# Batch 2 loaded transposed through memory, six output tiles split into half sums, and a new written order in a one-core attention + MLP kernel

## The chip, the cores and the metric

The kernel runs on one core of a Trainium2 chip. The metric is the device time of one execution in microseconds. One execution was also taken with the hardware profiler, and all the profile lines come from it. The engines are named as the profile names them: PE (TensorE, matrix products), PEld (its weight loads), DVE (VectorE), ACT (ScalarE), POOL (GpSimd, which here issues the casting loads) and SP (SyncE, which issues stores and transposed loads).

## The reference, cut to what matters

```python
# q, k, v: (8 batches, 12 heads, 448 positions, 64); w_in: (768, 2048); w_out: (2048, 768), all float32
scores = (1.0 / np.sqrt(64)) * np.matmul(q, k.transpose(0, 1, 3, 2))
m = np.max(scores, axis=-1, keepdims=True)
e = np.exp(scores - m)
attn = e / (np.sum(e, axis=-1, keepdims=True) + np.exp(-m) + 1e-09)
x = np.matmul(attn, v).transpose(0, 2, 1, 3).reshape(3584, 768)   # heads side by side
h = np.maximum(x @ w_in, 0.0)
out = (h * h) @ w_out                                             # (3584, 768) float32
```

The softmax has one more term, exp(0), in its denominator. The kernel computes exp(scores) without the maximum and adds 1 to the sum instead, which is the same quotient.

## The kernel before, in words

All matrix products are in float16, with sums in float32 in PSUM. Batches are worked on one after the other, and within a batch heads are taken four at a time, in a "quad": three quads a batch.

For each batch the kernel needs q and k with the head dimension on the partitions (tile `qk`, two buffers), so that scores come out with keys on partitions. There are two ways to get them:

- Batches in `ON_PE` (here 0, 1 and 2): POOL loads a quad of q and k in its natural layout, casting to float16 (`load_quad`, tiles `nn`); PE transposes it (`transpose_one`, 14 PE transposes a step, written `T b,g,n`); DVE or ACT copies the result to `qk` (`transposed_copy`, written `U`).
- The later batches: POOL copies all q and k of the batch to float16 tensors in device memory (`stage`), SP then loads them with a transposing DMA (`transposed_loads`, three planes: q, k, and k shifted by one row), and POOL picks the last 64 keys of every head out of the planes (`tail_keys`, four small copies).

In the second way the positions of a batch lie in another order, so `quad_scores` runs eight 64x64 products of 224 columns for a step instead of four of 448, `load_v_quads` takes four DMAs instead of one or three, and `store` writes rows with step 2 instead of 7.

A quad then goes through seven score steps (`s`), seven exps on ACT (`e`), DVE additions for the sums (`a`), a product with ones (`S`), logarithm and exp on ACT for the reciprocal (`Z`, `M`), seven products with the values (`v`), and two multiplications on DVE (`X`), which give x with its 768 features on the partitions (`xt`). Batch 0 does the same in halves of 224 queries (`p`, `b`, `y`, `z`, `n`, `x`, with `t`/`u`/`T`/`U` ahead of it).

The hidden layer takes x against w_in in 16 blocks of 128 features (`i` for batch 0 in pairs of blocks and halves of queries, `j` later), a relu on ACT or DVE (`r`, `k`), and a squaring on DVE (`g`, `l`) into the ring `gs`. An output tile is 128 tokens by 384 columns: 16 products of `gs` with w_out (`o`), then a scaled copy from PSUM (`O`) and a store on SP. `out_piece` has two forms: one 128x128 product a block, or (rows=True) four 64x64 products, whose two half sums lie in two PSUM banks, `op` and `lo`; then `out_first` (`O`) copies the one and `out_second` (`Q`, DVE, L563) adds the other.

Tile scheduling is by hand: the order of the instructions on every engine is the written one. It is a list of steps: `ORDER` (L662) for batches 0 to 2 with the first six output tiles (EARLY = 6), then `CYCLE` (L719) run five times for the later batches, then a tail of plain loops. Each engine takes its instructions in that order and waits where its data or its buffer is not ready. So a step that waits holds back all that stands behind it on its engine. That is so for the queues too: SP's stores and transposed loads are in one order, and POOL's loads, stage copies and tail copies are in one order.

The step `d n` issues `LOADS[n]` (L614). In `ORDER` of before these are the quads of batches 0, 1 and 2, the values, four parts of w_in, four of w_out, `stage(3)`, and `load_third` (transposed loads, tail copies and values of batch 3, `stage(4)`). In `CYCLE` a single `d0` near its end issues the transposed loads, tail copies and values of the next batch and the stage copies of the one after (`following`).

PSUM has two pairs of banks for scores (`s_psum`), and from the step `P0` on a ring of four banks (`ring`), which hidden-layer blocks, value products and output tiles take in turn. Output tiles in `ORDER` take one bank of it, those in `CYCLE` two. `osb_pool` has four buffers for copied output tiles.

Of the kernel before, what the change touches and what calls it, by code (L numbers as in the profile page):

```python
# [10 lines left out]
FP16 = mybir.dt.float16  # L11
# [5 lines left out]
def kernel(  # L17
# [9 lines left out]
    nc = tc.nc  # L27

    B, H, S, D = q.shape
# [4 lines left out]
    RUN = 4  # L34
    NQ = H // 4
    KC = S // 64
    ON_PE = (0, 1, 2)
    COLS = H * S // 2 + 16
    HALF = DM // 2
    FIRST = S // 2  # L40
# [11 lines left out]
    flat = ctx.enter_context(tc.tile_pool(name="flat", bufs=2))  # L52
# [90 lines left out]
    def stage(b):  # L143
        for n, t in (("q", q), ("k", k)):
# [11 lines left out]
            if hi < lo + TOTAL:  # L156
                nc.gpsimd.dma_start(out=st[hi - lo:TOTAL].rearrange("(r w) -> r w", r=1),
                                    in_=src[0:lo + TOTAL - hi].rearrange("(r w) -> r w", r=1))

    def transposed_loads(b):  # L160
        qk = qks[b] = qk_pool.tile([128, 3, COLS], FP16, name="qk")
        for i, n, x, c in ((0, "q", FRONT, H * S // 2), (1, "k", FRONT, H * S // 2), (2, "k", 0, COLS)):
            nc.sync.dma_start(
                out=qk[:, i, 0:c],
                in_=stages[n, b][x:x + c * 2 * D].rearrange("(r c) -> r c", c=2 * D),
                transpose=True,
            )

    kms = {}

    def tail_keys(b):

        km = kms[b] = flat.tile([128, H, 64], FP16, name="flatq")
        for r in range(2):
            for odd in range(2):
                rows_ = slice(64 * r, 64 * r + 64)
                which, x = (1, 0) if odd == r else (2, odd)
                src = qks[b][rows_, which, x:x + H * S // 2].rearrange("p (h x) -> p h x", h=H)
                nc.gpsimd.tensor_copy(km[rows_].rearrange("p h (x o) -> p h x o", o=2)[:, :, :, odd],  # L179
                                      src[:, :, S // 2 - 32:S // 2])  # L180
# [3 lines left out]
    def qk_of(b):  # L184
        if b not in qks:
            qks[b] = qk_pool.tile([128, 3, COLS], FP16, name="qk")
        return qks[b]
# [378 lines left out]
    def out_done(tok, n0, w, act=True):  # L566
        out_first(tok, n0, w, act)
        ot = ots.pop((tok, n0))
        del ops[tok, n0]
        store(tok, ot, n0, n0 + w)  # L570
# [28 lines left out]

    def load_quad(b, g):  # L600

        x = {(0, 1): (0, 0), (0, 2): (0, 1), (1, 0): (1, 0), (1, 1): (0, 0), (1, 2): (0, 1),
             (2, 0): (1, 0), (2, 1): (1, 1), (2, 2): (0, 0)}[b, g]
        if (b, x[0]) not in nats:
            nats[b, x[0]] = nat.tile([128, RUN * 2 * S], FP16, name=f"nn{x[0]}")
        load_natural_quads(b, (g,), x[1], nats[b, x[0]])

    def load_third():
        transposed_loads(3)
        tail_keys(3)  # L610
        load_v_quads(3)
        stage(4)

    LOADS = ([lambda b=b, g=g: load_quad(b, g) for b in range(3) for g in range(NQ) if b + g]  # L614
             + [lambda b=b, g=g: load_v_quads(b, g, g + 1) for b in range(2) for g in range(NQ)]
             + [lambda: load_v_quads(2)]
             + [lambda i=i: load_win(i, NW) for i in range(NW)]
             + [lambda n0=n0, y=y: load_wout(n0, y, 2) for n0 in (0, HALF) for y in range(2)]
             + [lambda: stage(3), load_third])

    def quad_visit(n):
        return divmod(n - N0, KC)
# [28 lines left out]
        "v": lambda m, c: values_step(m, c),  # L651
        "X": lambda m: quad_x(m),
        "P": lambda n: other_ring(),
        "o": lambda n, f0, f1: out_piece(128 * (n // 2), HALF * (n % 2), HALF, range(f0, f1)),
        "O": lambda n, act: out_done(128 * (n // 2), HALF * (n % 2), HALF, act),
    }

    def other_ring():
# [1 line left out]
        ring.append(ctx.enter_context(tc.tile_pool(name="ring", bufs=4, space=bass.MemoryType.PSUM)))  # L660

    ORDER = """  # L662
        d0 W8 c1,4,0 c0,0,1 c1,0,1 t0,0,0 c0,4,1 t1,0,0 u0,0,0,0 t1,0,4 u1,0,0,0 t0,0,4 u1,0,4,0 s0 d8 d1 u0,0,4,0 t0,1,0 e0 t1,1,0 u0,1,0,0 u1,1,0,0 s1 s2 e1
        d10 t0,1,4 u0,1,4,0 t1,1,4 u1,1,4,1 T0,1,0 T0,1,1 s3 U0,1,0,0,4,0 e2 U0,1,1,0,4,0 s4 U0,1,0,4,7,1 e3 d9 U0,1,1,4,7,0 d2 p0 e4 p2 s16 p1 e16 b0,0 b0,1
        p3 b0,2 b0,3 s6 y0 d18 s5 T0,2,0 e6 U0,2,0,0,4,0 z0 T0,2,1 U0,2,1,0,4,0 e5 U0,2,1,4,7,0 U0,2,0,4,7,0 s7 s9 b1,0 n0 b1,1 e7 x0 s8 p4 e9 b1,2 d3 b1,3 p5
        e8 p6 p7 s10 y1 b2,0 p8 p9 e10 s11 p10 b2,1 z1 e11 b2,2 b2,3 s12 p11 s13 n1 x1 y2 e12 T1,0,0 U1,0,0,0,7,0 T1,0,1 z2 n2 s14 e13 x2 p12 p13 s15
        U1,0,1,0,7,0 e14 e15 s17 p14 b3,0 b3,1 e17 s18 i0,7 d17 d5 b3,2 e18 b3,3 p15 y3 z3 b4,0 r0,7,0 s21 s19 e21 T1,1,1 d4 n3 b4,1 i0,6 U1,1,1,0,7,0 s20 d15
        T1,1,0 x3 b4,2 e19 b4,3 d16 s23 p16 p17 p18 r0,6,0 U1,1,0,0,7,0 e20 b5,0 e23 s22 e22 b5,1 p19 y4 s26 z4 n4 i0,4 g0,7 x4 r0,4,0 s27 i0,5 g0,6 b5,2 e26
        s25 e27 T1,2,1 s28 e25 p20 p21 r0,5,0 p22 s24 g0,5 b5,3 e28 d11 T1,2,0 p23 e24 s29 y5 e29 U1,2,1,0,7,0 U1,2,0,0,7,0 T2,0,0 T2,0,1 U2,0,0,0,7,0 z5 g0,4
        d6 U2,0,1,0,7,0 s30 n5 s32 a0,0 e30 d13 i0,0 i0,1 s33 x5 e32 r0,0,0 g0,0 r0,1,0 s31 i1,0 d12 g0,1 e33 i0,3 r1,0,0 e31 r0,3,1 s35 d7 s36 e35 P0 e36  # L670
        i0,2 s34 e34 a0,1 a0,2 g1,0 v0,0 a0,3 S0 v0,1 v0,2 v0,3 v0,4 Z0 v0,5 v0,6 M0 r0,2,0 g0,3 g0,2 s37 i1,3 a1,0 a1,1 e37 X0 r1,3,0 a1,2 g1,3 i1,6 s39 s40
        a1,3 e39 i1,1 r1,1,0 r1,6,0 s43 T2,2,0 e40 d20 T2,2,1 g1,6 e43 s42 g1,1 e42 U2,2,0,0,7,0 s41 d19 i1,5 r1,5,0 e41 s38 e38 T2,1,0 T2,1,1 U2,2,1,0,7,0
        U2,1,0,0,7,1 S1 a2,0 Z1 s44 U2,1,1,0,7,0 i1,4 i1,2 a2,1 e44 r1,4,1 s45 a2,2 g1,5 a2,3 v1,0 v1,1 M1 v1,2 v1,3 v1,4 v1,5 v1,6 r1,2,1 v2,0 S2 v2,1 X1
        g1,4 e45 g1,2 v2,2 v2,3 v2,4 Z2 v2,5 v2,6 M2 s47 X2 s46 i1,7 j3,0,2 r1,7,0 o0,0,4 j3,2,4 j1,0,2 j3,4,6 k3,0 j12,0,2 o0,4,8 j1,2,4 o0,8,12 e46 e47
        o0,12,16 s50 d21 g1,7 s51 j12,2,4 j1,4,6 k1,0 j5,0,2 e51 e50 l3 j5,2,4 j5,4,6 d23 O0,1 k5,1 j12,4,6 l5 o1,0,4 s48 s49 j6,0,2 e49 l1 e48 d22 k12,1 l12
        o1,4,8 o1,8,12 o1,12,16 s53 s52 e52 e53 j6,2,4 j10,0,2 o5,0,4 j6,4,6 O1,1 s55 k6,0 s54 j10,2,4 o5,4,8 j0,0,2 e55 a3,0 j10,4,6 j8,0,2 o5,8,12 j0,2,4
        a3,1 k10,1 o5,12,16 e54 s61 s57 l6 a4,0 j14,0,2 O5,0 e57 j14,2,4 j14,4,6 e61 j8,2,4 a3,2 j9,0,2 j9,2,4 j0,4,6 j9,4,6 a3,3 j8,4,6 l10 s56 k0,0 k14,0
        e56 l0 k8,1 s58 o2,0,4 o2,4,8 l14 d14 s59 v4,0 v4,1 v4,2 v4,3 a4,1 v4,4 v4,5 e58 k9,0 s60 e59 s64 o2,8,12 d24 l9 o2,12,16 a4,2 a4,3 j7,0,2 e60 v4,6
        e64 S4 Z4 M4 O2,0 S3 j7,2,4 o4,0,4 l8 o4,4,8 o4,8,12 o4,12,16 j7,4,6 Z3 s62 X4 s63 M3 O4,0 v3,0 v3,1 v3,2 v3,3 v3,4 v3,5 e62 v3,6 s65 X3 k7,1 j4,0,2
        e65 o3,0,4 a5,0 o3,4,8 o3,8,12 o3,12,16 j15,0,2 j4,2,4 j4,4,6 l7 e63 j15,2,4 a5,1 j2,0,2 O3,1 a5,2 j2,2,4 a5,3 j15,4,6 k4,0 j13,0,2 j11,0,2 S5 Z5  # L680
        k15,0 M5 l4 l15 j2,4,6 k2,0 j13,2,4 l2 j11,2,4 j13,4,6 j11,4,6 k11,1 k13,1 l11 l13
    """

    for step in ORDER.split():
# [4 lines left out]
    def cycle(b):  # L689
        m = NQ * (b - 1) - 1  # L690
        first = EARLY + KC * (b - 3)

        def following():
            if b + 1 < B:
                transposed_loads(b + 1)
                tail_keys(b + 1)
                load_v_quads(b + 1)
                if b + 2 < B:
                    stage(b + 2)

        return {
# [11 lines left out]
            "o": lambda n, f0, f1: out_piece(128 * ((first + n) // 2), HALF * ((first + n) % 2), HALF, range(f0, f1), True),  # L713
            "O": lambda n, act: out_first(128 * ((first + n) // 2), HALF * ((first + n) % 2), HALF, act),
            "Q": lambda n: out_second(128 * ((first + n) // 2), HALF * ((first + n) % 2), HALF),
            "d": lambda n: following(),
        }

    CYCLE = """  # L719
# [71 lines left out]
```

## Time and profile before

| | us |
|---|---|
| median of 3 runs | 396.94 (395.67 to 397.16) |
| the profiled execution | 396.87 |
| its span, first to last instruction | 394.8 |
| granted TensorE clock | 1.00 of full speed |
| ORDER ends (first value products of the first cycle) | 105.9 |
| five cycles, from one's first value products to the next's | about 45.2, one of them 46.3 |
| POOL waiting for transposed planes, ten waits | 205.6 |
| planes of batch 3: first issue, last plane landed | 83.6, 95.6 |

How to read it: the span is cut by the page into 40 slices of 9.9 us; a digit is the busy share of a slice in tenths. In a timeline a line gives the start, the length, the engine, the line of the kernel, the operation with its tiles and shapes, and how many instructions are merged; a bracket gives idle time ahead of it and what ended it. Matmuls overlap in the pipeline, so the length of one (about 0.32 us) is not its price; the price shows in the starts of a row of them. A window's line gives busy time of each engine, then the clock, the share of the DMA engines (above 1 when packets overlap) and GB/s.

### The profile page before, as it was taken

How to read it: one execution, taken by the hardware profiler on the slowest of the kernel's cores; microseconds unless marked ns; L12 is line 12 of the kernel's file. 1: busy time of each engine (PE TensorE's matmuls, PEld its weight loads, DVE VectorE, ACT ScalarE, POOL GpSimd, SP SyncE). 2: the span in 40 equal slices, each digit the busy share in tenths (PEclk: the TensorE clock that was granted, in tenths of full speed). 3: DMA queues.
4: the chain of work that ended last, by engine and by line, in shares of the span. 5: the costliest groups of instructions: out<-in, count | busy, mean ns of one | idle time of the engine just before them, and what ended most of it. 6: DMA issues, size and time to landing. Idle time of an engine off the chain costs nothing.

```text
span 394.8 us, 13877 instructions
## 1 busy us (share of the span) xinstructions
PE 385.5 (98%) x6252; PEld 262.9 (67%) x6252; DVE 240.5 (61%) x445; ACT 238.1 (60%) x324; POOL 59.8 (15%) x96
## 2 busy tenths in 40 slices
PE   8789999999999999999999999999999999999997
PEld 4567776445599766896579866776677765555665
DVE  3889994385746765668536876567646785285000
ACT  4999895768479625895279834896269934100111
POOL 8354500003200032000500016000500000000000
PEclk9999999999999999999999999999999999999999
DMA  8999999568942579419692398527652100100222
GB/s 146 203 204 206 203 206 208 98 127 154 191 85 63 113 140 181 96 43 161 113 203 75 77 193 127 129 64 141 126 74 68 58 7 2 62 0 14 68 80 81
DMA packets 75051, 45.33 MB, mean 115 GB/s; under 512 B 47472, under 2 KB 72944, under 8 KB 74992
## 3 DMA queue, kind: packets, MB, share of 16 engines
q0 software_dynamic: 24752, 22.62, 36.3%
q1 hardware_dynamic: 49952, 21.59, 25.0%
q8 instruction: 49, 0.80, 0.8%
q10 hardware_dynamic: 288, 0.23, 0.2%
q14 instruction: 10, 0.08, 0.1%
HBM read 45.69 MB, written 17.93 MB: 161 GB/s over the span
## 4 chain that ended last, share of the span: by engine, by line
PE 94%; DVE 3%; ACT 1%; issue 1%; DVEq 0%; ACTq 0%
PE mp L92 81%; PE sp L92 9%; PE xp L92 2%; PE mp L198 2%; ACT et L245 1%; DVE qk L208 1%; DVE half L334 1%; DVE half L332 0%; PE mp L225 0%; ACT rcp L356 0%; ACT rcp L363 0%; DVE qk L235 0%; DVE half L338 0%; DVE half L336 0%; DVE rt L496 0%
## 5 line engine op out<-in xcount | busy, mean ns | idle before, releaser
L92 PE MATMUL mp<-wout,gs 64*64 64x384 f16 (+2 forms) x2592 | 166.7, 322 | 0.0
L92 PE MATMUL mp<-xt,win 128*64 128x448 f16 (+2 forms) x1344 | 151.4, 339 | 0.1
L245 ACT ACTIVATE et<-sp 128x896 f16<-128x896 f32 (+1 forms) x131 | 110.8, 889 | 30.1 <-PE sp L92 28.9
L92 PEld LDWEIGHTS <-win 128*64 128x64 f16 (+1 forms) x1344 | 89.6, 106 | 58.7 <-issue 7.4
L92 PEld LDWEIGHTS <-gs 64*64 64x64 f16 (+1 forms) x2592 | 105.9, 106 | 34.3 <-issue 1.1
L494 ACT ACTIVATE rt<-mp 128x448 f16<-128x448 f32 x55 | 29.3, 544 | 57.2 <-PE mp L92 52.4
L500 DVE TENSOR_TENSOR gs<-rt 128x448 f16<-128x448 f16 x128 | 49.2, 401 | 22.2 <-ACT rt L494 19.8
L92 PE MATMUL sp<-qk 64*64 64x224 f16 (+1 forms) x1056 | 57.4, 274 | 2.5 <-issue 0.9
L496 DVE TENSOR_SCALAR rt<-mp 128x448 f16<-128x448 f32 x73 | 45.2, 621 | 23.0 <-PE mp L92 21.5
L557 ACT ACTIVATE ot<-mp 128x384 f32<-128x384 f32 (+2 forms) x34 | 16.4, 481 | 51.3 <-PE mp L92 50.8
L92 PEld LDWEIGHTS <-qk 64*64 64x64 f16 x1056 | 36.1, 114 | 14.4 <-issue 7.4
L179 POOL COPY flatq<-qk 64x384 f16<-64x384 f16 x20 | 12.4, 643 | 205.9 <-DMA qk<-stage_k 205.6
L245 ACT ACTIVATE nn<-sp 128x896 f16<-128x896 f32 x42 | 36.7, 915 | 1.9 <-PE sp L92 1.8
L478 DVE TENSOR_TENSOR xt<-mp,rcp 128x448 f16<-128x448 f32 x42 | 24.3, 620 | 20.0 <-ACT rcp L457 17.8
L92 PEld LDWEIGHTS <-vn 64*64 64x64 f16 x756 | 24.1, 107 | 9.8 <-issue 2.6
L563 DVE SCALAR_TENSOR_TENSOR ot<-mp,ot 128x384 f32<-128x384 f32 x35 | 19.5, 556 | 16.9 <-ACT ot L557 15.3
L454 ACT ACTIVATE rcp<-sp,one_b 128x896 f32<-128x896 f32 x21 | 21.2, 1007 | 10.0 <-PE sp L92 10.0
L92 PE MATMUL mp<-et,vn 64*64 64x448 f16 (+1 forms) x448 | 25.1, 343 | 0.0
L559 DVE TENSOR_SCALAR ot<-mp 128x384 f32<-128x384 f32 x23 | 12.8, 556 | 19.6 <-PE mp L92 19.5
L432 DVE TENSOR_TENSOR half<-et 128x1792 f16<-128x1792 f16 x15 | 16.3, 1087 | 7.0 <-ACT et L245 6.9
L457 ACT ACTIVATE rcp<-rcp 128x896 f32<-128x896 f32 x21 | 20.0, 952 | 0.6
L434 DVE TENSOR_TENSOR half<-half,et 128x1792 f16<-128x1792 f16 x15 | 16.4, 1091 | 0.7 <-ACT et L245 0.3
(59 smaller groups left out, 198.2 us busy)
## 6 DMA issues: line engine op xcount, KB each, us to landing
out_dram<-ot SPq DMA_DIRECT2D x52, 96.0 KB, 2.3
out_dram<-ot SPq DMA_DIRECT2D x19, 192.0 KB, 1.9
win<-in_moe_w_in_dram POOLq DMA_DIRECT2D x8, 384.0 KB, 11.1
wout<-in_moe_w_out_dram POOLq DMA_DIRECT2D x4, 768.0 KB, 15.6
vn<-in_v_dram POOLq DMA_DIRECT2D x10, 288.0 KB, 4.8
stage_q<-in_q_dram POOLq DMA_DIRECT2D x4, 676.0 KB, 8.8
stage_k<-in_k_dram POOLq DMA_DIRECT2D x4, 676.0 KB, 12.0
nn<-in_q_dram POOLq DMA_DIRECT2D x8, 224.0 KB, 8.1
```

The source lines that it names most:

```text
L92: return nc.tensor.matmul(out_, lhsT, rhs, start=start, stop=stop)
L245: nc.scalar.activation(out=out_, in_=in_, func=AF.Exp, scale=scale)
L432: nc.vector.tensor_add(esq[m], a[:, 0:w], a[:, w:2 * w])
L434: nc.vector.tensor_add(esq[m], esq[m], z[:, 0:w])
L454: nc.scalar.activation(out=rcp, in_=zp[:, :, 0:S], func=AF.Ln, bias=one_b)
L457: nc.scalar.activation(out=zqs[m], in_=zqs[m], func=AF.Exp, scale=-1.0)
L478: nc.vector.tensor_mul(xts[b][:, 2 * g + i, :], xqs[m][i][:, 0:S], zqs[m][:, i, :])
L494: nc.scalar.activation(out=rt[:, 0:m], in_=hp[:, 0:m], func=AF.Relu)
L496: nc.vector.tensor_scalar(out=rt[:, 0:m], in0=hp[:, 0:m], scalar1=0.0, scalar2=None, op0=ALU.max)
L500: nc.vector.tensor_mul(gs[:, f0:f0 + per, t0 % RING:t0 % RING + n], r, r)
L557: nc.scalar.activation(out=ot, in_=op[:, 0:w], func=AF.Copy, scale=OUT_SCALE)
L563: nc.vector.scalar_tensor_tensor(out=ot, in0=lo[:, 0:w], scalar=OUT_SCALE, in1=ot, op0=ALU.mult, op1=ALU.add)
```

## The change: what it does

Batch 2 leaves `ON_PE`. Its six T and six U steps and its three quad loads are gone; in their place `LOADS` gets `stage(2)` (d5) and `load_third(2)` (d6: three transposed loads on SP, four tail copies on POOL), and its values come in four DMAs. The six output tiles of `ORDER` are made as two half sums (`o` with rows=True, `O` as the first half, `Q` as the second). `ORDER` is written anew: steps of all kinds stand in other places, some copies and relus are on the other of ACT and DVE. In `CYCLE` the single step `d0` becomes seven: the three transposed loads after Q5, and after Q4 the two halves of the tail copies, the stage copies (d6) and the values (d5).

```diff
-    ON_PE = (0, 1, 2)
+    ON_PE = (0, 1)
...
+    PLANES = (("q", FRONT, H * S // 2), ("k", FRONT, H * S // 2), ("k", 0, COLS))
+
+    def transposed_load(b, i):
+        qk = qk_of(b)
+        n, x, c = PLANES[i]
+        nc.sync.dma_start(
+            out=qk[:, i, 0:c],
+            in_=stages[n, b][x:x + c * 2 * D].rearrange("(r c) -> r c", c=2 * D),
+            transpose=True,
+        )
+
     def transposed_loads(b):
...
+        for i in range(3):
+            transposed_load(b, i)
...
-    def tail_keys(b):
+    def tail_keys(b, planes=(1, 2)):
...
+        if b not in kms:
+            kms[b] = flat.tile([128, H, 64], FP16, name="flatq")
+        km = kms[b]
+        for which in planes:
+            for r in range(2):
                 rows_ = slice(64 * r, 64 * r + 64)
-                which, x = (1, 0) if odd == r else (2, odd)
+                odd, x = (r, 0) if which == 1 else (1 - r, 1 - r)
...
+    def load_third(b):
+        transposed_loads(b)
+        tail_keys(b)
+        if b == 3:
+            load_v_quads(b)
+            stage(b + 1)
+
+    LOADS = ([lambda b=b, g=g: load_quad(b, g) for b in ON_PE for g in range(NQ) if b + g]
+             + [lambda: stage(2), lambda: load_third(2)]
+             + [lambda b=b, g=g: load_v_quads(b, g, g + 1) for b in ON_PE for g in range(NQ)]
              + [lambda: load_v_quads(2)]
              + [lambda i=i: load_win(i, NW) for i in range(NW)]
              + [lambda n0=n0, y=y: load_wout(n0, y, 2) for n0 in (0, HALF) for y in range(2)]
-             + [lambda: stage(3), load_third])
+             + [lambda: stage(3), lambda: load_third(3)])
...
-        "o": lambda n, f0, f1: out_piece(128 * (n // 2), HALF * (n % 2), HALF, range(f0, f1)),
-        "O": lambda n, act: out_done(128 * (n // 2), HALF * (n % 2), HALF, act),
+        "o": lambda n, f0, f1: out_piece(128 * (n // 2), HALF * (n % 2), HALF, range(f0, f1), True),
+        "O": lambda n, act: out_first(128 * (n // 2), HALF * (n % 2), HALF, act),
+        "Q": lambda n: out_second(128 * (n // 2), HALF * (n % 2), HALF),
...
     ORDER = """
+        d0 c0,0,1 c1,0,1 W8 c1,4,0 c0,4,1 t0,0,0 u0,0,0,0 t1,0,0 u1,0,0,0 t1,0,4 t0,0,4 s0 u1,0,4,1 t0,1,0 u0,0,4,1 u0,1,0,0 e0 t1,1,0 u1,1,0,0 s1 s2
+        t0,1,4 t1,1,4 d1 d7 d8 e1 e2 d9 u0,1,4,0 s13 u1,1,4,0 T0,1,0 s14 e13 s12 e14 T0,1,1 e12 U0,1,0,0,4,0 U0,1,0,4,7,0 s3 T0,2,1 b0,0 U0,1,1,0,4,0
...
+        s23 d5 e22 i0,1 b4,1 x3 b4,2 s20 r0,0,0 b4,3 p16 e23 p17 p18 r0,1,0 s27 e20 p19 y4 b5,0
...
+        d12 s37 i1,4 e37 i1,3 a1,2 s39 s41 r1,4,1 g1,0 e39 g1,4 i0,5 r0,5,0 e41 r1,3,1 i1,2 a1,3 s40 s38 d6 d21 e40 i1,1 e38 g0,5 s42 e42 o0,0,4 s43
+        e43 g1,3 o0,4,8 s44 o0,8,12 o0,12,16 e44 a2,0 S1 r1,2,0 r1,1,1 Z1 g1,2 a2,1 i1,7 r1,7,1 O0,0 g1,1 Q0 v1,0 d20 v1,1 M1 v1,2 a2,2 a2,3 v1,3 v1,4
+        v1,5 v1,6 v2,0 S2 v2,1 v2,2 v2,3 Z2 v2,4 M2 v2,5 X1 v2,6 s56 X2 s52 o2,0,4 o2,4,8 g1,7 o2,8,12 o2,12,16 e56 e52 s57 O2,0 s53 j4,0,2 j0,0,2 d22
...
+        o4,8,12 o4,12,16 s49 e58 s50 k10,1 l10 O4,1 j8,0,2 j3,0,2 j11,0,2 j3,2,4 e49 j11,2,4 j8,2,4 j8,4,6 e50 j3,4,6 s48 k8,1 Q4 s45 j5,0,2 a4,0 l8
...
+        a4,2 s60 k12,0 o3,8,12 k13,1 o3,12,16 o5,0,4 e60 s64 o5,4,8 s51 e64 a3,0 d23 a4,3 e51 o5,8,12 O3,0 o5,12,16 S4 Q3 v4,0 l12 v4,1 v4,2 v4,3 Z4
...
-        def following():
+        def following(n):
             if b + 1 < B:
-                transposed_loads(b + 1)
-                tail_keys(b + 1)
-                load_v_quads(b + 1)
-                if b + 2 < B:
+                if n < 3:
+                    transposed_load(b + 1, n)
+                elif n < 5:
+                    tail_keys(b + 1, (n - 2,))
+                elif n == 5:
+                    load_v_quads(b + 1)
+                elif b + 2 < B:
                     stage(b + 2)
...
     CYCLE = """
...
+        v1,2 v1,3 M1 v1,4 O5,0 v1,5 Q5 d0 d1 d2 v1,6 X1 o6,0,2 s3,4 e3,4 o6,2,4 s3,0 e3,0 o6,4,6 o6,6,8 a2,0 o6,8,10 o6,10,12 s3,1 o4,0,2 o6,12,14
+        a2,1 s3,3 e3,1 o4,2,4 o6,14,16 s3,2 e3,3 o4,4,6 O6,1 a2,2 o4,6,8 s3,5 a2,3 o4,8,10 Q6 o4,10,12 e3,2 e3,5 o4,12,14 o4,14,16 O4,1 Q4 d3 d4 d6 d5
```

In the new numbering of `LOADS`, d0 to d4 are the quads of batches 0 and 1, d7 to d12 the values of batches 0 and 1, d13 those of batch 2, d14 to d17 w_in, d18 to d21 w_out, d22 `stage(3)` and d23 `load_third(3)`. POOL meets them in this order: d0 d1 d7 d8 d9 d2 d3 d14 d17 d15 d16 d4 d18 d10 d5 d19 d11 d12 d6 d21 d20 d22 d13 d23. In the step names, quads are numbered from batch 1 on, and the score steps from 24 on: s45 to s51, s52 to s58 and s59 to s65 (with their e) are the three quads of batch 2, and v3, v4, v5 its values.

## The prediction

> **What bounds the kernel now.** I read the page first: engine totals, the 40 slices, the chain that ended last.
>
> ```profile
> span 394.8 us, 13877 instructions
> PE 385.5 (98%) x6252; PEld 262.9 (67%) x6252; DVE 240.5 (61%) x445; ACT 238.1 (60%) x324; POOL 59.8 (15%) x96
> PE   8789999999999999999999999999999999999997
> DMA  8999999568942579419692398527652100100222
> PE 94%; DVE 3%; ACT 1%; issue 1%; DVEq 0%; ACTq 0%
> ```
>
> TensorE is 94% of the chain and never idle for long after the second slice, so a change pays by taking work from TensorE, or costs by making it wait. The second limit is the DMA row: full for the first seven slices, about 70 us.
>
> Next the TensorE timeline, to price its work.
>
> ```profile
> 54.56 0.97 PE L198 MATMUL mp<-ident,nn 128*64 128x128 f16 x28
> 55.47 0.38 PE L92 MATMUL sp<-half,ones 64*64 64x448 f16 x4
> ...
> 63.47 0.81 PE L92 MATMUL mp<-wout,gs 128*128 128x384 f16 x4
> 64.12 1.68 PE L92 MATMUL mp<-xt,win 128*128 128x448 f16 x8
> 66.66 1.46 PE L92 MATMUL mp<-wout,gs 128*128 128x384 f16 x8
> 68.06 0.57 PE L92 MATMUL sp<-qk 64*64 64x448 f16 x8
> 68.56 1.69 PE L92 MATMUL mp<-xt,win 128*128 128x448 f16 x8
> ...
> 119.96 1.51 PE L92 MATMUL mp<-wout,gs 64*64 64x384 f16 x32
> 121.26 0.59 PE L92 MATMUL sp<-qk 64*64 64x224 f16 x16
> ```
>
> Here start minus next start is the price. Four 128x384 matmuls take 0.65 us (0.162 each); eight before scores take 1.40, so a change from full array to 64x64 tiles costs 0.10; two scores of 0.19 take 0.50 before full-array work, so the way back costs 0.12. Two step T's (28 transposes) take 0.91 with one such change, so one T is 0.39.
>
> I summed the written order (ORDER) with these prices. Before: 16 T 6.24, 66 scores 12.0, 16 i 18.4, 48 j 18.1, 24 o 15.6, values, sums, first transposes and warming 15.7, 66 changes of tile form 7.6: 93.65 us. The trace stands behind this sum by 11.6 us at the first hidden-layer step (24.6 us), by 12.1 at 45 us, and by 12.26 at the end of ORDER (105.9 us). So all idle time of this stretch lies in the first 25 us, where ACT is full (5.00 of 5 us in two 5-us windows), and what follows runs at the price of its matmuls.
>
> **The change, part by part.**
>
> *Six T of batch 2 go:* 6 x 0.39 = 2.34 us of TensorE, on the path. The scores of batch 2 become eight 64x224 in place of four 64x448: 0.19 us in both forms (121.26 to 121.64 for two), nothing.
>
> *The new order* has 57 changes of form, not 66: 17 x 0.10 into 64x64 from the full array, 18 x 0.125 back, 22 x 0.12 with the 128x64 form, 6.59 us, so 1.0 us less. Together ORDER holds 90.30 us, 3.35 less.
>
> *Six output tiles as half sums:* 16 chunks at 0.162 in both forms (32 matmuls from 119.96 to 121.26 are eight chunks): nothing on TensorE. DVE gets six second halves of 0.556 (L563), 3.3 us, and loses five copies of 0.62 (ACT loses one of 0.91): even. Cover gone, each would cost its 0.56. Each tile holds two of the ring's four banks. At the three tightest places of the new order (v1,0 after O0; j11,0 after O4; o3,0 after k11) a bank is asked for 1.3 to 1.5 us of TensorE work after its last matmul, and needs one release of 0.49 to 0.62; the old order lived with 1.23 (o2,0 after k0). Bounds 0 and 6 x 0.56 = 3.3; I take 0.
>
> *The start* is reordered: e13, e14, e12 come before the second quad's scores, and four copies change between ACT and DVE. Summing ACT's work up to each exp in the written order (0.86 an exp) and taking off TensorE's work before it, the largest surplus, which TensorE must idle, is 7.5 us in the new order and 7.7 in the old: 0.2 less; two ACT copies that now run before the first exp save up to 1 more. I take 11.8 us of idle in place of 12.1; ends 10.6 and 12.3.
>
> *Batch 2's loads.* Gone from POOL: six casting loads (0.73 us of issue each); new: two stage copies (0.60 each), four tail copies (0.61), three more loads of values; POOL is idle 85%, so this costs nothing itself. But the three transposed loads sit between: SP waits for both stage copies, POOL's tail copies wait for the planes, and behind them on POOL stand d21, d20 (wout), stage(3), v(2). And TensorE's s56 needs all three planes. This is the one new wait, and I work out when they land.
>
> ```profile
> 83.60 2.40 SPq L163 DMA_TRANSPOSE qk<-stage_q  x1
> 86.10 5.88 SPq L163 DMA_TRANSPOSE qk<-stage_k  x2
> 91.39 0.61 POOL L179 COPY flatq<-qk 64x384 f16<-64x384 f16 x1 [42.93 <-DMA qk<-stage_k]
> 95.56 1.82 POOL L179 COPY flatq<-qk 64x384 f16<-64x384 f16 x3 [3.56 <-DMA qk<-stage_k]
> q0 software_dynamic: 11395, 10.62, 118.1%
> 85.00:87.00 2.00, 2.00 (x18) 0.85 (x17) 1.72 (x5) 1.18 (x2) 0.00 (x0) 1.00 1.20 264
> ```
>
> These are the SP and POOL timelines, POOL's queue in 20 to 75 us, and a 2-us window (last number GB/s). POOL's loads alone fill the engines; so do transposed loads alone (1.20, 264). POOL's loads move 204 GB/s, or 199 KB a us, from 10 us on, where 1,436 KB are done. That puts the old stage_k, 12,328 KB down the queue, at 64.7; it landed at 66.3 (45.03 plus 21.3), so 1.6 us is the lag. In the new order stage_k ends at 9,000 KB: 48.0, landed 49.6; three loads behind it (wout, two of v) bring 10,216 KB: 54.1. The planes are 2.07 MB; four windows from 85 to 93 us average 246 GB/s: 8.4 us of full engines. Since nothing is left over, all is done at 54.1 + 8.4 + 1.6 = 64.1. Were the planes alone, they would land 9.5 us after the first k issue (86.10 to 95.56): 59.1. I take 64.1, nearest to the row in which SP's 96 KB stores took 7.1 us instead of 2.3 beside POOL's copies (99 to 110 us): SP's traffic comes off worse.
>
> [...]
>
> s56 stands after 50.8 us of TensorE work, due at 50.8 + 11.8 = 62.6: a wait of 1.5 us. After it 39.5 us of work follow, and 0.2 of small waits as in the old order: ORDER ends at 64.1 + 39.7 = 103.8 instead of 105.9: 2.1 us gained.
>
> What stands behind: after the tail copies POOL's 3,560 KB (d21, d20, stage(3), v(2)) move from about 67 us on, 17.9 us, so v(2) lands near 86.5, and v4,0 comes 25.6 us of TensorE work after s56, at 89.7. wout's second half lands near 76 and o3,0 comes at 83.6. SP's first store (O0) waits up to 3 us behind the transposes; ot has four buffers. d23's transposes stand ahead of Q3's and Q5's stores, the same.
>
> *The cycles.* Transposed loads start after Q5's store, about 19 us into a cycle, not 28.6; the old ones end with a tail copy at 147.0 and are first used at 152.5. They are hidden before and after: 0. Stores O6 and O4 wait for 8.3 us of SP issue, covered by ot's buffers. One gap of 0.88 us (TensorE, 162.4, ended by no event) may go or return: 0, ends -0.9 and +0.9.
>
> *Sum:* the profiled execution took 396.87 us (span 394.8 and 2.07 around it; the median is 396.94, of 395.67 to 397.16). 396.87 - 2.1 = 394.8.
>
> **The rivals.**
>
> *The planes come in time* (up to 62.6): 3.35 + 0.3 stay, 393.3; with the best start 392.1. For it: transposed loads alone land at 59.1. Against: full engines. 0.19.
>
> *Planes late but not ruinous*, at 65.5 to 68.2: the gain ends at 66.2 (105.9 - 39.7), so 396.2 to 398.9. 0.14.
>
> *Slower: transposed loads starve beside POOL's loads.* Place: s56. Each us past 66.2 costs one; past 68.2 it is slower by over 0.5%. Doubling the 9.5 us gives 49.6 + 19 = 68.6, 399.3. For it: the store at 7.1 for 2.3 us; against: only 6 us of other loads lie behind stage_k. 0.14.
>
> *Ring waits* take the place of the removed work: 3.3 us back, 398.1. The gaps of 1.3 us are short but exceed the release. 0.08.
>
> *Weight loads show in the 64x64 tiles:* 96 chunks with one load of 107 ns bare would be 10.3 us, 405. The rows at 119.96 (0.162 a chunk) leave no room for that. 0.02.
> [...]
>
> **How the numbers follow.** My forecast, planes at 62.6 to 65.5, has 0.43: 393.3 to 396.2, likeliest 394.8. Against 396.94, 0.5% (about what can be told from no change) is 2.0 us: below 394.95 faster, above 398.9 slower. Faster: 0.25 of the 0.43, 0.19, and a little of the rest: 0.45. Slower: 0.14, half of the ring's 0.08, 0.02: 0.20. Same: 0.35. The range reaches from the best start (392.1, less 0.3 for the gap) to the starved planes: 391.8 to 399.3.
>
> **What would show it.** After: T steps of batch 2 gone; ORDER's end (the cycle's first values) near 103.8; TensorE idle 1 to 2 us before the first 64x224 score of batch 2 near 64, and the first of its tail copies on POOL near 61 to 64. Wrong if no wait stands there (faster), if the wait exceeds 5 us, if v4,0 or an o waits, or if the idle before 25 us grew.

## The result, and the profile after

The changed kernel takes 399.19 us (median of 6 runs, 398.10 to 399.76) against 396.52 us (6 runs, 395.67 to 397.16) for the kernel before on the same chip: a ratio of 1.0068, with a 95% interval of 1.0048 to 1.0088. It is slower by 2.7 us, where 2.1 us of gain were forecast. The profiled execution took 399.27 us.

The page of the changed kernel: span, slices of TensorE, granted clock and DMA, and the shares of the chain.

```profile
span 397.5 us, 14465 instructions
...
PE   8899995999999999999999999999999999999996
...
PEclk9999997899999999999999999999999999999999
DMA  9999998999892989168932999259602100100232
...
PE 89%; DMA 3%; ACT 2%; DVE 2%; SPq 2%; issue 1%; POOL 1%; DVEq 0%; POOLq 0%; ACTq 0%
```

Two digits tell most of it. TensorE has a 5 in the seventh slice (59.6 to 69.6 us), where before had a 9, and the clock has a 7 and an 8 in the seventh and eighth, where before had full speed throughout. The chain, which had no DMA and no SP before, now runs through SP's queue (6.5 us at 54 to 61 us) and the last two planes (5.86 us, to 66.6).

The timeline of TensorE after, around that place and at the end of ORDER:

```profile
60.19 1.30 PE L92 MATMUL mp<-et,vn 64*64 64x448 f16 x24
64.34 0.30 PE L92 MATMUL sp<-qk 64*64 64x224 f16 x1 [2.85 <-DMA qk<-stage_k]
66.64 0.96 PE L92 MATMUL sp<-qk 64*64 64x224 f16 x15 [2.00 <-DMA qk<-stage_k]
67.21 5.37 PE L92 MATMUL mp<-wout,gs 64*64 64x384 f16 x64
72.33 0.64 PE L92 MATMUL sp<-qk 64*64 64x224 f16 x16
...
109.28 1.49 PE L92 MATMUL mp<-nn,vn 64*64 64x448 f16 x28
```

The first line is the last v of quad 2. It is done near 61.3, and there s56 comes due: the first score step of batch 2. Its first matmul, which needs only the first two planes, waits until 64.34, the other fifteen until 66.64. So TensorE stands for 5.3 us with one matmul in between. Then o2's 64 matmuls take 5.12 us (67.21 to 72.33); eight such chunks cost 1.30 in the trace of before, so sixteen should cost 2.60. Why they take double is in the windows of the same trace (length, busy TensorE, clock, DMA share, GB/s):

```profile
65.00:66.00 1.00, 0.00 (x0) 0.74 1.27 289
66.00:67.00 1.00, 0.36 (x8) 0.50 1.02 217
71.00:72.00 1.00, 1.00 (x19) 0.50 1.30 202
72.00:73.00 1.00, 1.00 (x28) 0.85 1.31 204
```

The granted clock falls to half while TensorE stands, and stays there until after 72 us. So the wait is paid twice: once as idle time, and again as work at half speed.

The balance at the end of ORDER (109.28 us; before 105.91): 3.35 us less work, 1.6 us less idle time in the start (s56 due at 61.3 after 50.8 us of work, 10.5 us of idle time where before had 12.1), 5.3 us of waiting for the planes, and 2.6 us of low clock (2.52 in o2, the rest in the scores ahead of it): -3.35 - 1.6 + 5.3 + 2.6 = +2.95, against 3.37 measured. The 0.4 left over is put down to small waits; one of them, about 0.25 us for a bank of the ring near 107 us, is in the trace. From there to the end of the span it is 288.2 us after and 288.9 before: the cycles are 0.7 shorter. The 0.88 us gap of before's second cycle is not there; the first three cycles take 45.72, 45.17 and 45.17 (before 45.23, 46.34 and 45.34).

Why the planes come late, in the timelines of SP and POOL and in the shares of the two DMA queues from 50 to 55 us (q0 is POOL's, q1 SP's):

```profile
46.34 8.64 SPq L165 DMA_TRANSPOSE qk<-stage_q  x1
55.03 9.56 SPq L165 DMA_TRANSPOSE qk<-stage_k  x2
64.44 1.26 POOL L187 COPY flatq<-qk 64x384 f16<-64x384 f16 x2 [26.62 <-DMA qk<-stage_k]
66.65 1.28 POOL L187 COPY flatq<-qk 64x384 f16<-64x384 f16 x2 [0.94 <-DMA qk<-stage_k]
```

```profile
q0 software_dynamic: 941, 0.74, 93.0%
q1 hardware_dynamic: 863, 0.22, 33.0%
qk<-stage_q SPq DMA_TRANSPOSE x1, 14.2
```

The first transposed load holds SP for 8.64 us; the one of batch 3 in the kernel before, with no other loads beside it, held it 2.40. It lands after 14.2 us instead of 5.4 (the median of five in before). In these five microseconds each queue got about the same number of packets, 941 and 863, but a packet of POOL's loads carries 0.74 MB / 941 = 790 bytes and one of the transposed loads 255. So with nearly equal counts SP's queue moved 0.22 MB of 0.96, less than a quarter. The counts are not that close everywhere: from 84 to 90 us, when the planes of batch 3 ran beside POOL's loads, it was 1368 packets (0.90 MB) for POOL and 618 (0.31 MB) for SP.

When POOL's loads are done, near 57 us, the planes have the engines alone, and still two holes appear (same columns of windows, without TensorE):

```profile
59.00:60.00 1.00, 1.00 0.05 5
63.00:64.00 1.00, 1.00 0.40 33
```

Before the second and before the third plane little or nothing moves for over a microsecond. In the second of these holes TensorE already stands and waits for just these planes.

### The profile page after: what moved, and what is told of

It reads as the page before. It is cut to its first block, busy times and chain, and to the rows that moved or that the text cites. A ratio compares the mean times of both kernels' runs of the same rounds, so it can differ in the third digit from the quotient of the medians.

```text
span 397.5 us, 14465 instructions
## 1 busy us (share of the span) xinstructions
PE 385.4 (97%) x6540; PEld 259.2 (65%) x6540; DVE 239.4 (60%) x442; ACT 239.7 (60%) x327; POOL 62.9 (16%) x99
## 4 chain that ended last, share of the span: by engine, by line
PE 89%; DMA 3%; ACT 2%; DVE 2%; SPq 2%; issue 1%; POOL 1%; DVEq 0%; POOLq 0%; ACTq 0%
PE mp L92 78%; PE sp L92 9%; DMA nn<-in_k_dram 2%; SPq L165 2%; DMA qk<-stage_k 1%; ACT et L253 1%; PE mp L206 1%; PE xp L92 1%; POOL nn L116 1%; DVE half L342 0%; DVE xt L486 0%; ACT rcp L462 0%; DVE half L440 0%; ACT rcp L465 0%; DVE gs L508 0%
## 5 line engine op out<-in xcount | busy, mean ns | idle before, releaser
L92 PEld LDWEIGHTS <-win 128*64 128x64 f16 (+1 forms) x1344 | 91.2, 106 | 57.5 <-issue 6.6
L92 PEld LDWEIGHTS <-gs 64*64 64x64 f16 (+1 forms) x2880 | 102.0, 108 | 35.6 <-issue 0.9
L502 ACT ACTIVATE rt<-mp 128x448 f16<-128x448 f32 x59 | 31.4, 543 | 64.3 <-PE mp L92 52.5
L92 PE MATMUL sp<-qk 64*64 64x224 f16 (+1 forms) x1116 | 54.5, 267 | 6.7 <-DMA qk<-stage_k 4.8
L504 DVE TENSOR_SCALAR rt<-mp 128x448 f16<-128x448 f32 x69 | 42.6, 620 | 16.7 <-PE mp L92 15.5
L187 POOL COPY flatq<-qk 64x384 f16<-64x384 f16 x24 | 17.0, 710 | 198.8 <-DMA qk<-stage_k 157.6
L92 PEld LDWEIGHTS <-qk 64*64 64x64 f16 x1116 | 34.4, 116 | 20.2 <-issue 5.8
L486 DVE TENSOR_TENSOR xt<-mp,rcp 128x448 f16<-128x448 f32 x42 | 24.3, 619 | 20.9 <-ACT rcp L465 20.4
L571 DVE SCALAR_TENSOR_TENSOR ot<-mp,ot 128x384 f32<-128x384 f32 x41 | 22.8, 555 | 17.1 <-ACT ot L565 13.3
L92 PEld LDWEIGHTS <-vn 64*64 64x64 f16 x756 | 22.4, 107 | 10.4 <-issue 1.3
## 6 DMA issues: line engine op xcount, KB each, us to landing
stage_k<-in_k_dram POOLq DMA_DIRECT2D x5, 676.0 KB, 11.8
```

The costliest lines, as they stand in the source:

```text
L92: return nc.tensor.matmul(out_, lhsT, rhs, start=start, stop=stop)
L486: nc.vector.tensor_mul(xts[b][:, 2 * g + i, :], xqs[m][i][:, 0:S], zqs[m][:, i, :])
L502: nc.scalar.activation(out=rt[:, 0:m], in_=hp[:, 0:m], func=AF.Relu)
L504: nc.vector.tensor_scalar(out=rt[:, 0:m], in0=hp[:, 0:m], scalar1=0.0, scalar2=None, op0=ALU.max)
L571: nc.vector.scalar_tensor_tensor(out=ot, in0=lo[:, 0:w], scalar=OUT_SCALE, in1=ot, op0=ALU.mult, op1=ALU.add)
```

## The experiments

The theory after the result: (1) the planes' wait alone would have left the kernel near where it was, and the half clock that follows it makes it slower; (2) the place of the scores, not the new form of the work, is what loses; (3) the half sums, the planes and the cycle are free or pay. Rivals: the low clock comes from something else at this place (the half sums, 64x64 products beside full DMA); the loads' order in the queues is at fault; the new cycle loses. In the shared runs the kernel before took 396.54 us (7 runs, first four experiments) and 396.47 us (16 runs, last four).

**Filling the wait with idle products.** `f26` issues 26 products of a constant, 128x128 by 448, into a bank that nobody reads: work of the same length as most of the wait. Nothing of the computation is left out.

```diff
-        ... X1 v2,6 s56 X2 s52 o2,0,4 ...
+        ... X1 v2,6 f26 s56 X2 s52 o2,0,4 ...
```

> The changed kernel with 26 idle matmuls (128x448 columns, about 4.9 us, results unused) ahead of s56, where TensorE otherwise stands idle. Theory (the wait for batch 2's planes idles TensorE, and the idle time itself halves its clock): the planes still land near 66.6 us and s56 runs no earlier, but the granted clock stays 1.00 from 65 to 72 us and the 64 matmuls of o2 take 2.6 us instead of 5.1; ORDER ends near 106.7 instead of 109.3 and the time is 399.2 - 2.5 = 396.7 us. Rival (the low clock has another cause: the 64x64 tiles that follow, or the full DMA engines): clock 0.5 at 66 to 72 us again and 399 us or more.

Measured: 398.67 us (398.40 to 398.81), ratio 1.0058 (1.0037 to 1.0079). Its TensorE timeline, and three windows:

```profile
61.79 5.17 PE L92 MATMUL mp<-const-bfloat16-1.0 128*128 128x448 bf16 x26
66.89 0.98 PE L92 MATMUL sp<-qk 64*64 64x224 f16 x16
67.61 2.86 PE L92 MATMUL mp<-wout,gs 64*64 64x384 f16 x64
70.22 0.64 PE L92 MATMUL sp<-qk 64*64 64x224 f16 x16
...
93.07 1.53 PE L92 MATMUL mp<-et,vn 64*64 64x448 f16 x28
94.39 0.49 PE L92 MATMUL sp<-qk 64*64 64x224 f16 x10
96.28 0.40 PE L92 MATMUL sp<-qk 64*64 64x224 f16 x6 [1.40 <-issue]
```

```profile
65.00:66.00 1.00, 1.00 (x7) 1.00 1.27 290
66.00:68.00 2.00, 1.91 (x30) 1.00 0.93 204
68.00:70.00 2.00, 2.00 (x59) 1.00 0.00 0
```

The same half sums, now at 1.00, take 67.61 to 70.22 = 2.61 us. That settles the cause of the slow o2: the standing, and not the tile form. Full DMA engines are not the cause either: from 65 to 66 us their share is 1.27 in both kernels, and the clock falls in the changed one alone (0.74 there, 1.00 here). In time, neither expectation was met (396.7, or 399 and more): of the 2.5 us only 0.5 reached the total, so this run does not show that the low clock costs the whole kernel 2.6 us, and with a clock of 1.00 in all four executions it is still 2.1 us slower than the kernel before. Up to the values step v4 the gain is there: v4 starts at 93.07, in the changed kernel at 95.17, although the planes landed 0.64 later (POOL's last tail copies start at 67.29, not 66.65). Then, at 94.9 to 96.3, a gap of 1.40 us stands inside one score step, ended by nothing that the profile shows, like the 0.88 of before's cycle, and the first cycle's values come at 109.06, 0.2 earlier than in the changed kernel. What made that gap is open.

**Scores of batch 2 later.** s56, s52, s57 and s53 move behind o2, j4 and j0, 5.4 us of work.

```diff
-        ... v2,6 s56 X2 s52 o2,0,4 o2,4,8 ... e56 e52 s57 O2,0 s53 j4,0,2 j0,0,2 d22 j0,2,4 ...
+        ... v2,6 X2 o2,0,4 o2,4,8 ... O2,0 Q2 j4,0,2 j0,0,2 d22 j0,2,4 j0,4,6 j4,2,4 j4,4,6 s56 s52 e56 e52 s57 s53 j9,0,2 ...
```

> The changed kernel with the first four score steps of batch 2 (s56, s52, s57, s53 with their exps) moved behind o2, j4 and j0, that is behind 5.1 us more of TensorE work. Theory (5.3 us of wait and 2.6 us of low clock are the whole loss): s56 comes due near 66.5 us, at which the planes have landed, so wait and low clock both go; ORDER ends near 101.7 instead of 109.3; time 399.2 - 7.6 = 391.6 us, below the kernel before (396.5). Rival (the scores are now late for what hangs on them: exps of batch 2 reach the value steps v4 and v3 late, and less hidden-layer work is left to fill): up to 5 us come back as waits between 85 and 105 us, 394 to 397 us.

Measured: 399.06 us (397.73 to 399.85), ratio 1.0075 (1.0048 to 1.0102): nothing gained in the time, though the wait is gone. TensorE's timeline and windows show where it went (this execution, 397.73 us, is the fastest of the four):

```profile
68.26 0.40 PE L92 MATMUL sp<-qk 64*64 64x224 f16 x8 [0.82 <-ACT et L253]
...
91.30 1.33 PE L92 MATMUL mp<-et,vn 64*64 64x448 f16 x24 [1.54 <-DVE ot L571]
93.28 0.58 PE L92 MATMUL mp<-et,vn 64*64 64x448 f16 x2 [0.65 <-DMA vn<-in_v_dram]
```

```profile
92.00:93.00 1.00, 0.63 (x16) 1.00 0.39 65
93.00:94.00 1.00, 0.72 (x14) 0.50 1.27 283
96.00:97.00 1.00, 1.00 (x6) 0.80 1.87 239
97.00:98.00 1.00, 1.00 (x9) 1.00 1.14 19
```

TensorE came to v4, the first use of batch 2's values for its second quad, while those were still on their way: issued from 70.9 us on, they need 18.1 to 20.4 us. The first of the two waits is put down to a copy on DVE, but the weight loads of the values waited 3.0 us for that transfer. And once more the clock fell, here for 3.4 us. In the changed kernel this transfer is as late (issued from 70.7 on, the last at 72.7 and 20.4 us on its way, so 93.1), and hides only because TensorE is late too: v4 starts at 95.17.

**Three other loads ahead.** The loads that ran beside the planes (d19, d11, d12: wout and two of values) move ahead of batch 2's stage copies.

```diff
-        ... s23 d5 e22 ... e32 d19 T1,2,1 ... a1,1 d11 d12 s37 ...
+        ... s23 d19 d11 d12 d5 e22 ... e32 T1,2,1 ... a1,1 s37 ...
```

> The changed kernel with the three POOL loads that stood behind stage(2) (a part of w_out, two of v) issued ahead of it, so that nothing else is in flight while the planes load. Theory (the planes were slowed by these loads: SP needed 8.6 us to issue the first plane instead of 2.4): stage copies land 6 us later, near 52.4 and 55.7 us, SP's first issue takes 2.4 to 3.2 us, and the last plane lands 9.5 us after the first k issue, near 65.2 instead of 66.6; the wait shrinks by 1.4 us, the clock still drops, time near 397.8 us. Rival (batch 2's planes are slow by themselves, 20.3 us from first issue to last landing as in the changed kernel): last landing near 72.7 us, wait 11 us, time near 405 us.

Measured: 399.43 us (399.22 to 399.78), ratio 1.0079 (1.0057 to 1.0100). SP and POOL:

```profile
53.14 4.73 SPq L165 DMA_TRANSPOSE qk<-stage_q  x1
57.93 6.76 SPq L165 DMA_TRANSPOSE qk<-stage_k  x2
66.75 1.29 POOL L187 COPY flatq<-qk 64x384 f16<-64x384 f16 x2 [0.75 <-DMA qk<-stage_k]
```

The planes start 6.8 us later, hold SP for 11.5 us instead of 18.2, and land at the same time to 0.1 us. What the planes lose beside POOL's loads they gain after them. Neither expectation was met (65.2 and 397.8 us, or 72.7 and 405). A hole is here too (120 GB/s from 62 to 64 us, with 255 and 253 in the two microseconds on either side). That fits a landing set by the bytes of both queues and the holes, whatever their order; only this one other order was tried.

**The six tiles as full-array products.** The new order with the old form of the output tiles, one 128x128 product a block and one bank.

```diff
-        "o": lambda n, f0, f1: out_piece(128 * (n // 2), HALF * (n % 2), HALF, range(f0, f1), True),
-        "O": lambda n, act: out_first(...),
-        "Q": lambda n: out_second(...),
+        "o": lambda n, f0, f1: out_piece(128 * (n // 2), HALF * (n % 2), HALF, range(f0, f1)),
+        "O": lambda n, act: out_done(...),
+        "Q": lambda n: None,
```

> The changed kernel with only the six early output tiles as before (16 products of the full array into one bank, no second half). Theory (the half sums cost nothing themselves, and save changes of tile form where o stands beside scores and values): 28 more changes at 0.10 or 0.125 us, 3.15 us, so ORDER ends near 112.4 instead of 109.3 and the time is near 402.3 us. Rival (half sums cost waits for the second bank and DVE's second half, 0.56 us each): the tiles as before give 3.3 us back, and the two cancel, 399 us or less.

Measured: 401.43 us (400.45 to 402.25), ratio 1.0127 (1.0097 to 1.0157), 2.2 us above the changed kernel; the first cycle's values come at 112.01 instead of 109.28. The half sums pay. ORDER ends 2.73 us later without them, where 28 more changes of tile form were summed to 3.15; that the changes are the whole of it is not shown apart. The clock falls here too (at 65.4 us), with no half sums in ORDER.

**Scores later, and the values ahead.** The second experiment with the transfer that it uncovered moved: after the tail copies POOL issues one part of wout and then batch 2's values, ahead of the other part and of batch 3's stage copies; pieces of j9 stand between the score steps.

```diff
-        ... s38 d6 d21 e40 ... v1,0 d20 v1,1 ... v2,6 s56 X2 s52 o2,0,4 ... d22 j0,2,4 ... o3,0,4 d13 e46 ...
+        ... s38 d6 d20 d13 d21 d22 e40 ... v1,0 v1,1 ... v2,6 X2 o2,0,4 ... j4,4,6 s56 s52 e56 e52 j9,0,2 j9,2,4 s57 j9,4,6 k4,1 j10,0,2 s53 ... o3,0,4 e46 ...
```

> The changed kernel with the scores of batch 2 moved behind o2, j4 and j0 as in the run with later scores, and two more moves for what took the gain there: v(2) goes ahead of the second half of w_out and of stage(3) on POOL's queue, and j9 stands between the second and third of the moved scores. Theory (in the run with later scores, v(2) landed only at 91 to 93 us, TensorE stood before v4 and lost its clock again, some 4 us; 1.2 us went to exps): v(2) lands near 79 us, v4 doesn't wait, the clock is 1.00 throughout, ORDER ends near 102.5 us, time near 392.3 us, below the kernel before (396.5). Rival (the next transfer in line takes over: the planes of batch 3 now start 3.4 us later and land after the first cycle asks for them, near 104 us): the gain stays between 0 and 3 us, 396 to 399 us.

Measured: 393.81 us (5 runs, 392.63 to 395.03), ratio to the kernel before 0.9933 (0.9899 to 0.9966). It beats both kernels. Its TensorE timeline, and windows over the rest of ORDER:

```profile
66.62 0.59 PE L92 MATMUL sp<-qk 64*64 64x224 f16 x15 [0.24 <-DMA qk<-stage_k]
...
102.37 1.49 PE L92 MATMUL mp<-nn,vn 64*64 64x448 f16 x28
```

```profile
60.00:66.00 6.00, 6.00 (x96) 1.00 1.25 220
66.00:72.00 6.00, 5.60 (x85) 1.00 0.73 117
72.00:90.00 18.00, 18.00 (x339) 1.00 1.27 204
90.00:102.00 12.00, 11.97 (x167) 1.00 1.14 193
```

The planes land at 66.6, as late as ever, but s56 is only then due. The values need 8.1 to 9.0 us in place of 18.9 to 20.4. TensorE is busy to 0.43 us in 42, the clock stays at 1.00, and ORDER ends 6.9 us earlier than in the changed kernel, 3.5 earlier than before. The profiled execution is the fastest of the five (392.63 us); by the medians the gain over the kernel before is 2.7 us. That is the gain that the change had in it.

**Half of the wait.** The scores behind o2 only, with the values ahead. Is there a price of the clock when the wait is short?

```diff
-        ... s38 d6 d21 e40 ... v1,0 d20 v1,1 ... v2,6 s56 X2 s52 o2,0,4 o2,4,8 g1,7 o2,8,12 o2,12,16 e56 ... d22 j0,2,4 ... o3,0,4 d13 e46 ...
+        ... s38 d6 d20 d13 d21 d22 e40 ... v1,0 v1,1 ... v2,6 X2 o2,0,4 o2,4,8 g1,7 o2,8,12 o2,12,16 s56 s52 e56 ... j0,2,4 ... o3,0,4 e46 ...
```

> The changed kernel with the scores moved behind o2 alone (2.6 us of work), and v(2) ahead as in the run beside it. TensorE's wait for the planes shrinks from 5.3 to about 2.7 us. Theory (the clock falls only after an idle time between 2.7 and 5 us): granted clock 1.00 after the wait, j4 and j0 at 0.19 us a matmul, 5.1 us gained of the wait and the clock, time near 394.1 us. Rival (any wait of some microseconds costs the clock): clock 0.5 for 5 us after it, only the 2.6 us of wait gained, time near 396.6 us.

Measured: 397.99 us (397.49 to 399.68), ratio 1.0043 (1.0022 to 1.0064). TensorE and windows:

```profile
64.73 0.29 PE L92 MATMUL sp<-qk 64*64 64x224 f16 x1 [0.42 <-DMA qk<-stage_k]
67.05 0.96 PE L92 MATMUL sp<-qk 64*64 64x224 f16 x15 [2.02 <-DMA qk<-stage_k]
...
69.97 5.27 PE L92 MATMUL mp<-xt,win 128*128 128x448 f16 x19
```

```profile
66.00:67.00 1.00, 0.00 (x0) 0.62 1.15 249
67.00:68.00 1.00, 0.95 (x15) 0.50 0.86 183
72.00:73.00 1.00, 1.00 (x5) 0.50 1.31 204
73.00:74.00 1.00, 1.00 (x7) 0.96 1.31 203
```

A wait of 2.4 us in two pieces costs as long a stretch of half clock as one of 5.3: from 66.2 to 73.1 us. The 24 matmuls of j4, j0, j9 and j10 take 6.15 us (69.97 to 76.12) instead of 4.65. So the price was no fixed share of the wait: 6.83 us of half clock in both. The time is above both expectations (394.1 and 396.6): besides the low clock TensorE stood 0.64 and 0.22 us for exps of the moved scores.

**The new cycle alone.** The kernel before, with only the new `CYCLE` and the split steps of `following`.

```diff
-        ... v1,5 Q5 v1,6 X1 o6,0,2 ... Q4 a3,0 s3,6 ... S3 Z3 d0 l14 M3
+        ... v1,5 Q5 d0 d1 d2 v1,6 X1 o6,0,2 ... Q4 d3 d4 d6 d5 a3,0 s3,6 ... S3 Z3 l14 M3
```

> The kernel before with only the new places of the loads in the cycle (transposed loads after Q5, tail copies, stage copies and values after Q4). Theory (hidden in both places; only the gap of 0.88 us in the second cycle may go, as it went in the changed kernel, where the cycles took 0.85 us less): 395.6 to 396.5 us, all five cycles at 45.1 to 45.4 us. Rival (the new places collide with the stores or with the value loads): a cycle over 45.6 us, 397 us or more.

Measured: 395.60 us (10 runs, 394.92 to 397.22), ratio 0.9987 (0.9972 to 1.0003): no difference that can be told. It is not what loses.

**The values ahead, scores in place.** The changed kernel with the order of POOL's loads of the fifth experiment and nothing else.

```diff
-        ... s38 d6 d21 e40 ... v1,0 d20 v1,1 ... d22 j0,2,4 ... o3,0,4 d13 e46 ...
+        ... s38 d6 d20 d13 d21 d22 e40 ... v1,0 v1,1 ... j0,2,4 ... o3,0,4 e46 ...
```

> The changed kernel with only v(2) moved ahead of the second half of w_out and of stage(3). Theory (in the changed kernel v(2) landed at 93.1 us, 2 us before v4 asked for it, because TensorE was already late by the wait for the planes): no change, 399.2 us, the wait at s56 and the low clock as they were. Rival (v(2) or the loads behind it were a bound of their own): 398 us or less, or o3 waits for w_out and the time is above 400 us.

Measured: 399.90 us (398.50 to 400.13), ratio 1.0082 (1.0061 to 1.0104), no better than the changed kernel. Each move alone (this and the second experiment) brings nothing; both together, with the pieces of j9 between the score steps, bring 5.4 us; what those pieces add was not run by itself. They are two waits one behind the other, and whoever takes the first away meets the second.

## Why the prediction was wrong, by its steps

*The removed work* was right. No T of batch 2 is left, the scores in their new form cost the same (0.19 us a step, two from 102.20 to 102.58), and the half sums cost nothing on TensorE (0.163 us a chunk in the first experiment); with full tiles the same order is 2.2 us slower. From s56's fifteen matmuls (66.64) to the end of ORDER it is 42.64 us; without 2.6 of low clock and a ring wait of 0.25 this is 39.8, against 39.5 forecast.

*The start* was priced too dear. I took 11.8 us of idle time, with 10.6 as the best end; it was 10.5. Since s56 must wait for its planes in any case, this only made the wait longer.

*The landing of the planes* is the first term that was mis-sized: 64.1 forecast, 66.64 measured, 2.5 us. The bytes and the end of POOL's loads were near enough; but I moved 2.07 MB at a mean of windows with full engines, and the planes do not fill the engines. There is a hole ahead of the second and of the third, about 1.4 us each (5 GB/s from 59 to 60 us, 33 from 63 to 64), and the trace of before has one too (94 to 95 us, 13 GB/s, behind the four windows that I averaged). I read a mean from the stretch without the hole. With an earlier due time the wait became 5.3 us, not 1.5. By my own rivals a landing at 66.64 is "late but not ruinous", and that rule gave 66.64 + 39.7 = 106.3 at the end of ORDER, or about 397.3 us: no difference that can be told.

*The clock* is the step that is missing, and by the balance of the trace it decided the sign. I priced a late plane at one microsecond a microsecond ("each us past 66.2 costs one"). The trace of before could not warn of more: its clock is 1.00 throughout, its longest single gap 0.88 us while there is work. But a wait of a few microseconds was exactly what I forecast as new, and I took the clock as given. The first experiment shows that the same matmuls take 2.6 us instead of 5.1 once TensorE is kept busy. The terms then close: 103.8 forecast, + 2.5 for the planes, + 2.6 for the clock, + 0.3 rest = 109.2, against 109.28. In the total the sign is not shown to hang on the clock, since that experiment kept the clock and stayed slower, with a new gap of 1.40 us. What is shown is that the kernel is faster than before once TensorE stands neither for the planes nor for the values (fifth experiment).

*Whether a shorter wait would have been harmless* can't be read from the longest gap: in the changed kernel no stretch of standing before the fall is longer than 2.85 us, in the sixth experiment none is longer than 1.22, and there two pieces of 1.64 us together came before it. My wait of 1.5 us lies between the 1.41 us that no fall followed and those 1.64 (last section), so what it would have cost is not shown.

*SP's share beside POOL's loads.* I took the slow stores for a sign that SP's traffic comes off worse, and from 50 to 55 us it did: 863 packets and 0.22 MB against POOL's 941 and 0.74. From 84 to 90 us it was 618 and 0.31 against 1368 and 0.90. The bytes were uneven in both stretches, the counts in the second.

*What stands behind.* I put the values of batch 2 at 86.5, 3 us ahead of their use; they landed at 93.1. From 83.7 us on they ran beside the transposed loads of batch 3 (SP, 83.7 to 99.0), which I had left out of that sum. It showed in no wait of the changed kernel, only because TensorE was late, and it ate the gain of the second experiment.

*The cycles* (0, ends -0.9 and +0.9) came out at -0.7; alone they make no difference that can be told. *The ring* showed a wait of about 0.25 us near 107 us, not 3.3. The rivals on the ring and on weight loads fell: sixteen 64x64 chunks took 2.61 us at full clock (first experiment), the price of 0.162 each that I had read from before.

So of the rivals, "transposed loads starve beside POOL's" named the place, s56, and the slow first plane (14.2 us to its landing). That the starving set the landing of the last plane, the third experiment speaks against. Its point of decision was wrong: 68.2 us was the price without the clock, and 66.6 was enough. That the measured 399.19 us lies beside its 399.3, the upper end of my range, is luck: the 399.3 stood for a landing at 68.6 and a full clock.

## What to carry to other kernels

In six executions here TensorE stood for 1.64 us or more out of 3.41, and 3.41 or 6.83 us of half clock followed. When a change puts a wait of that size before TensorE, price the wait and then a stretch of work at half clock behind it, and look at the clock of the windows before looking at anything else. A transfer that is late by a few microseconds can be met by moving its first use behind other work, but look at the next transfer in the same queue in the same sitting: here the first move alone (399.06 us) and the second alone (399.90) gave nothing, and both together 393.81. Where two queues share the engines, compare the bytes of a packet (here 790 against 255) before assuming that they share evenly.

## What the runs showed of the hardware

Read in tenths of a microsecond, in each of six executions the clock falls from 1.00 to 0.50 in one step and comes back in one step, and the time between is 3.41 us or twice that:

| kernel | falls at | returns at | length | TensorE idle in the 3.41 us ahead of the fall |
|---|---|---|---|---|
| after | 65.48 | 72.31 | 6.83 | 3.1 |
| three loads ahead | 65.60 | 72.42 | 6.83 | 3.1 |
| full tiles | 65.45 | 72.27 | 6.83 | 2.4 |
| half of the wait | 66.24 | 73.07 | 6.83 | 1.64 |
| values ahead alone | 66.84 | 73.67 | 6.83 | 3.1 |
| scores later | 92.99 | 96.41 | 3.41 | 1.90 |

The last column is worked out from the timelines; for half of the wait it is 0.42 + 1.22 (65.02 to 66.24). The clock record of the changed kernel begins at 4.04 us, and its later changes come 18, 20 and 115 times 3.413 us after that: the fall, the return, and the fall after the last matmul. That of the kernel before begins at 6.10 us, and its one fall, after the last matmul, comes 114 times 3.413 us later. Other stretches of the same length, counted off from these times and from the falls of the other kernels, held less idle time, added up, and no fall followed them: 1.35 us in the second experiment (65.69 to 69.10), 1.40 in the start of the kernel before (12.92 to 16.34) and 1.41 in the eighth (60.01 to 63.43). Nor did one follow the gap of 1.40 us in the first experiment (94.88 to 96.28). For the return the numbers are others: TensorE stood for 1.0 to 1.95 us of the first 3.41 us of half clock in the five long cases, and the clock stayed low for as long again; in the short one it stood for 0.28. These are few cases. What follows an idle time between 1.41 and 1.64 us no run shows, and no run was made to test it. The length of the low clock can differ from one execution to the next: the mean clock of the changed kernel is 0.990 or 0.991 in five of its six executions and 0.996 in the sixth. By an estimate from its span of 397.5 us, 6.83 us of half clock leave a mean of 0.991 and 3.41 us leave 0.996.

The other thing is the two holes between transposed loads (5 GB/s and an engine share of 0.05 from 59 to 60 us, 33 GB/s and 0.40 from 63 to 64), with SP already issuing the next load (55.03 to 64.59). What makes them is open, and so is the gap of 0.88 or 1.40 us inside a score step that no event ends. Both gaps fall into stretches in which the DMA moves next to nothing: 19 GB/s from 161.5 to 162.4 us in the kernel before, 6 GB/s from 94.70 to 95.35 in the first experiment. The changed kernel has such a stretch at the same place (7 GB/s from 94.5 to 95.5) and no gap in it, so the two need not come together.
